# Where the first token columns come from, who casts the weights, and the order of the first FFN pieces

## The chip, the cores and the metric

The kernel runs on one core of one Trainium2 chip. The metric is the device time of one execution in microseconds (us), and lower is better. An execution is called slow here when it is over 1.5% above the fastest one of the same kernel; ratios use fast runs alone. "The profile" is one execution recorded by the hardware profiler. PE is TensorE, DVE is VectorE, ACT is ScalarE, POOL is GpSimd, SP is SyncE; a q after a name (SPq, ACTq) is that engine issuing a DMA.

## The reference, cut to what matters

```python
# q, k, v: (8 batches, 8 heads, 576 tokens, 64), float32
q_s = softmax(q, axis=features)
k_s = softmax(k, axis=tokens)
kv  = einsum('bhsd,bhde->...', k_s, v)      # one 64x64 matrix per batch and head
x   = einsum('bhsd,bhde->bhse', q_s, kv)    # reshaped to 4608 tokens x 512

logits = x @ w_gate + modality_bias[modality_id]    # 8 experts
e_idx  = argmax(logits)
out    = prob[e_idx] * (relu(x @ w1[e_idx]) @ w2[e_idx])   # 512 -> 1024 -> 512
```

With this draw of inputs the modality bias decides, and only two experts get tokens. The kernel finds the two from the bias at run time, and has a loop for any others that does nothing here.

## The kernel before: the parts that the argument touches

Each batch goes through four steps. Attention makes x. Routing chooses the expert and works out a row number (`place`) for each token. Five *sends* by GpSimd write the token rows into a table `xd` in memory, sorted by expert from both ends. A *fetch* by SP reads 256 rows of the table back, transposed, as the columns `xt` that the FFN multiplies.

```python
def fetch(ph):                                   # ph is the batch
    for slot, lo, w in todo_of(ph):              # two passes: slot 0 and slot 1
        xt, d = fetch_x(lo, w)                   # SP, transposing DMA: xt <- xd
        after(d, part_of[ph], "rows are sent before they are read")
        ti, d = fetch_info(lo, w)                # SP, small rows: gate and token id
        ...
        got[lo] = (xt, ti)

def main_pieces():                               # the FFN, as one stream of pieces
    late = []
    for ph in range(NPH):
        for slot, lo, w in todo_of(ph):
            xt, ti = got.pop(lo)
            ...
            yield from ffn1(w, slot, xt, hT)     # 4 pieces: h_ps, 8 products each
            late.append((ph, lo, w, slot, hT, ti))
            if len(late) > 1 or (ph, slot) == (0, 0):
                yield from second(*late.pop(0))  # 4 pieces: y_ps, 4 products each
```

`mains(n)` emits the next n pieces. `weave(side, rate)` runs attention and routing, and after each of their steps adds `rate` times the step's weight to an account; for each whole unit in it one piece is emitted. The order in which instructions are emitted is the order in which an engine runs them:

```python
alone(route(0)); fetch(0)
cast_weights(0, 0, nc.scalar)
load_weights(eids[1], 1, nc.scalar, (0, 1))      # second expert, from ACT
... attention 1, casts, loads of parts 2 and 3 ...
alone(route(1)); fetch(1)
cast_weights(0, 3, nc.scalar)
load_batch(2, "k", nc.scalar)
cast_weights(1, 0, nc.scalar)
cast_weights(1, 1, nc.vector)
load_batch(2, "v", nc.scalar)
mains(4)
cast_weights(1, 2, nc.scalar)
load_batch(2, "q", nc.scalar)
mains(2)
cast_weights(1, 3, nc.vector)
mains(4)
p2 = prep(2, nc.scalar)
for _ in range(6):
    mains(1); next(p2, None)                     # 16 pieces so far
weave(chain(attend(2), route(2)), 0.6, prep(3, nc.scalar), 6)
fetch(2)
weave(chain(attend(3), route(3)), 0.5, prep(4, nc.scalar), 4)
for b in range(4, B):
    fetch(b - 1)
    weave(chain(attend(b), route(b)), 0.97, ...)
```

A batch has 16 pieces. Because the second product of a pass runs one pass late, piece 13 is the first that needs the fetched rows of batch 1, and piece 29 the first that needs those of batch 2. Before, 16 pieces stand ahead of attention 2 and 25 ahead of attention 3.

The softmax here doesn't subtract the row's maximum and nothing guards it: scores larger than these inputs give would overflow.

## Time and profile before

| | before |
|---|---|
| median of 3 runs | 283.08 us (281.9 to 288.72) |
| span of the first profile; granted TensorE clock | 275.2 us; 0.93 |
| TensorE busy | 192.0 us, 70% of the span |
| kvT of batch 1 (end of the first hole) | 42.63 us |
| first FFN product | 51.25 us |
| first product of batch 1's rows; wait before it | 66.76 us; 2.6 us |
| logits of batch 3; wait for the third fetch just ahead of them | 108.69 us; 8.6 us |

Times of day count from the span's start. The lines themselves are in the prediction. A timeline line has start, duration, engine, source line, operation, tiles and count; in brackets stand the idle time of the engine before it and what ended it.

Before was profiled a second time near the end of the study: span 277.7 us, of the fast state, clock 0.94. Below, "the second profile of before" is this one.

### The profile page before, as it was taken

What the parts mean: (1) busy time and instruction counts of PE and PEld (TensorE: products, weight loads), DVE (VectorE), ACT (ScalarE), POOL (GpSimd) and SP (SyncE); (2) the same over time, 40 slices, a digit from 0 to 9 for tenths busy, and PEclk for the clock granted to TensorE, in tenths of its full rate; (3) what the DMA queues carried; (4) which work ended last, traced back from release to release, by engine and by line L of the source; (5) the groups of instructions that cost most, each with busy time, mean ns of one, the idle gap of its engine ahead of it and who ended that gap; (6) DMA issues with size and microseconds to landing.
All of it is one profiled execution on the core that took longest, in us unless ns stands there. A gap on an engine that the chain in (4) does not pass through costs nothing.

```text
span 275.2 us, 4856 instructions
## 1 busy us (share of the span) xinstructions
PE 192.0 (70%) x1769; PEld 131.3 (48%) x1790; DVE 128.3 (47%) x434; ACT 117.6 (43%) x153; POOL 97.0 (35%) x150
## 2 busy tenths in 40 slices
PE   0255604596996714799899289979989879999700
PEld 0244504464664403556656055746746556665400
DVE  1456805840268510964864445485694202223420
ACT  2268503655977151738358016912513333331100
POOL 7040610651034510370406725256347512223400
PEclk9999999998998975999999759999999999999975
DMA  7999999999987797399978762913613693211200
GB/s 182 361 380 403 392 409 285 279 321 248 312 312 254 293 304 159 128 346 263 163 278 278 295 112 82 156 62 109 156 48 119 139 220 108 79 76 71 78 18 0
DMA packets 46170, 56.94 MB, mean 207 GB/s; under 512 B 27227, under 2 KB 27243, under 8 KB 46140
## 3 DMA queue, kind: packets, MB, share of 16 engines
q10 hardware_dynamic: 11104, 25.43, 27.1%
q1 hardware_dynamic: 30076, 16.39, 25.4%
q0 software_dynamic: 4960, 14.74, 15.4%
q8 instruction: 16, 0.26, 0.4%
q14 instruction: 14, 0.11, 0.1%
HBM read 36.84 MB, written 15.25 MB: 189 GB/s over the span
## 4 chain that ended last, share of the span: by engine, by line
PE 45%; DMA 22%; DVE 18%; issue 5%; ACT 3%; POOL 1%; SPq 0%; another core or an unknown queue 0%; DVEq 0%; POOLq 0%; ACTq 0%
PE h_ps L664 20%; PE y_ps L681 15%; DMA xt<-xd 9%; DMA xd<-xb,place 5%; DMA st<-in_q_dram 5%; DVE xb L462 4%; PE tp_ps L388 3%; DMA st<-in_moe_w_dram 3%; PE kv_ps L355 2%; DVE y_sb L691 2%; PE x_ps L451 2%; PE lg_ps L417 2%; ACT et L316 2%; DVE lg L483 1%; POOL xd L564 1%
## 5 line engine op out<-in xcount | busy, mean ns | idle before, releaser
L664 PE MATMUL h_ps<-xt,W 128*128 128x256 bf16 (+1 forms) x640 | 81.0, 284 | 22.8 <-DMA xt<-xd 20.0
L671 ACT ACTIVATE hT<-h_ps 128x512 bf16<-128x512 f32 x76 | 44.8, 599 | 84.7 <-PE h_ps L664 75.5
L664 PEld LDWEIGHTS <-W 128*128 128x128 bf16 x640 | 61.7, 104 | 35.6 <-DMA xt<-xd 12.6
L681 PE MATMUL y_ps<-W,hT 128*128 128x512 bf16 x283 | 72.1, 382 | 1.2 <-issue 0.2
L694 POOL DMA_INDIRECT out_dram<-y_sb,ix x38 | 38.3, 1007 | 74.7 <-DVE y_sb L691 61.1
L691 DVE TENSOR_SCALAR y_sb<-y_ps,ti 128x512 f32<-128x512 f32 x38 | 28.5, 750 | 51.0 <-PE y_ps L681 46.0
L564 POOL DMA_INDIRECT xd<-xb,place x40 | 39.7, 992 | 30.8 <-DVE et L318 10.0
L681 PEld LDWEIGHTS <-hT 128*128 128x128 bf16 x304 | 27.7, 98 | 27.4 <-issue 0.6
L462 DVE TENSOR_TENSOR xb<-x_ps,qi 128x512 bf16<-128x512 f32 (+1 forms) x40 | 25.6, 675 | 2.9 <-PE x_ps L451 2.6
L451 PE MATMUL x_ps<-kvbd,et 128*128 128x128 bf16 (+1 forms) x160 | 17.6, 253 | 7.5 <-DVE xb L462 7.5
L355 PE MATMUL kv_ps<-vb,ek 64*128 64x129 bf16 x288 | 13.4, 244 | 12.0 <-DVE vb L318 12.0
L336 ACT ACTIVATE eq<-st 128x1152 bf16<-128x1152 f32 x16 | 18.5, 1170 | 5.7 <-DMA st<-in_q_dram 5.7
L336 ACT ACTIVATE ek<-st 128x1152 bf16<-128x1152 f32 x16 | 17.9, 1158 | 4.2 <-DMA st<-in_k_dram 4.2
L451 PEld LDWEIGHTS <-et 128*128 128x128 bf16 (+1 forms) x160 | 12.6, 116 | 13.7 <-DVE xb L462 8.5
L509 POOL TENSOR_TENSOR na<-valid,isa 128x5 f32<-128x5 f32 x8 | 1.6, 199 | 47.6 <-DVE isa L498 47.6
L355 PEld LDWEIGHTS <-ek 64*128 64x128 bf16 x288 | 10.2, 108 | 16.7 <-issue 16.4
L388 PE MATMUL tp_ps<-ident,eq 128*128 128x128 bf16 x144 | 13.3, 242 | 6.2 <-DVE kvbd L376 3.1
L316 ACT COPY et<-tp_ps 128x1024 bf16<-128x1024 bf16 x8 | 8.1, 1012 | 19.0 <-PE tp_ps L388 19.0
L316 ACT CAST vb<-st 128x1152 bf16<-128x1152 f32 x14 | 15.9, 1153 | 0.0
L388 PEld LDWEIGHTS <-eq 128*128 128x128 bf16 x144 | 10.5, 109 | 11.2 <-ACT eq L336 3.4
L316 ACT CAST W<-st 128x2048 bf16<-128x2048 f32 x6 | 11.3, 1892 | 0.0
L408 PE MATMUL g_ps<-wg_sb,kvT 128*128 128x8 bf16 x32 | 2.0, 169 | 12.7 <-ACT kvT L404 12.7
(111 smaller groups left out, 134.8 us busy)
## 6 DMA issues: line engine op xcount, KB each, us to landing
st<-in_k_dram ACTq DMA_DIRECT2D x6, 1152.0 KB, 6.9
st<-in_v_dram ACTq DMA_DIRECT2D x6, 1152.0 KB, 9.7
st<-in_q_dram ACTq DMA_DIRECT2D x6, 1152.0 KB, 8.3
st<-in_moe_w_dram SPq DMA_DIRECT2D x4, 1024.0 KB, 15.1
st<-in_moe_w_dram ACTq DMA_DIRECT2D x4, 1024.0 KB, 13.4
st<-in_k_dram SPq DMA_DIRECT2D x2, 1152.0 KB, 9.5
st<-in_v_dram SPq DMA_DIRECT2D x2, 1152.0 KB, 12.8
st<-in_q_dram SPq DMA_DIRECT2D x2, 1152.0 KB, 14.2
```

What stands on the lines that cost most here:

```text
L316: nc.scalar.copy(out=out, in_=in_)
L336: nc.scalar.activation(out=view((eks if nm == "k" else eqs)[b], [[Dh, 2], [HG * Dh, NJ], [1, Dh]], 2 * g * Dh), in_=src[:, 2 * g : 2 * g + ...
L355: nc.tensor.matmul(out=kv[hg][:, 130 * hp : 130 * hp + 129], lhsT=ek[rows, j, P * hp : P * hp + P], rhs=vb[rows, j, hp, 0:129], start=(j = ...
L388: nc.tensor.transpose(out=view(tp, [[2 * nj * 64, 2], [1, 64]], hp * nj * 64 + jj * 64), in_=eq[:, c0 + jj, P * hp : P * hp + P], identity ...
L451: nc.tensor.matmul(out=view(x_ps, [[2 * Dh, 2], [1, Dh]], (4 * (p_ % 2) + p_ // 2) * Dh, (0, T)), lhsT=et[:, p_, tcol[t] : tcol[t] + T], r ...
L462: nc.vector.tensor_tensor(out=view(xb, [[2 * Dh, HG], [Dh, 2], [1, Dh]], t * RW, (0, T)), in0=view(x_ps, [[2 * Dh, HG], [Dh, 2], [1, Dh]], ...
L564: w = nc.gpsimd.indirect_dma_start(out=xd, out_offset=bass.IndirectOffsetOnAxis(ap=place[0:T, t : t + 1], axis=0), in_=xb[0:T, t, :], in_o ...
L664: nc.tensor.matmul(out=h_ps[:, f * w : (f + 1) * w], lhsT=W[:, slot, kd * F + (f0 + f) * P : kd * F + (f0 + f + 1) * P], rhs=xt[:, kd, 0:w ...
L671: nc.scalar.activation(out=hT[:, f0 : f0 + nf, 0:w], in_=view(h_ps, [[w, nf], [1, w]]), func=ACT.Relu)
L681: nc.tensor.matmul(out=y_ps, lhsT=hT[:, kf, t * P : (t + 1) * P], rhs=W[:, slot, W2 + kf * D : W2 + (kf + 1) * D], start=(kf == 0), stop=( ...
L691: nc.vector.tensor_scalar(out=y_sb, in0=y_ps, scalar1=gate[:, t, 3:4], scalar2=None, op0=ALU.mult)
L694: store = nc.gpsimd.indirect_dma_start(out=out, out_offset=bass.IndirectOffsetOnAxis(ap=ix[:, t : t + 1], axis=0), in_=y_sb, in_offset=Non ...
```

## The change

The intent: the first two FFN passes need not wait for the trip of batch 0's rows through memory, since the rows are still in on-chip memory. A 0/1 matrix built from the row numbers, multiplied from the right, sorts and transposes them at once. ACT no longer issues weight loads, which held its queue for 9 us. Casts are spread over three engines. The order of pieces around attention 2 is changed with it.

```diff
+    def sort_first():
+        xb = xb_b[0]
+        for side in range(2):
+            xt = xpass.tile([P, KD, GW], BF16, name="xt"); firsts.append(xt)
+            ... for half, kd, t: 40 products
+                nc.tensor.matmul(out=s_ps[:, kd, :], lhsT=xb[0:T, t, ...],
+                                 rhs=perms[side][0:T, t, :], ...)
+            copy_on(nc.vector if half else nc.scalar, xt[...], s_ps)
 # in route, ahead of the sends:
+        if ph == 0:
+            ... pl2 = place, as floats, once for each side
+            for side in range(2): for t in range(NT):
+                nc.vector.tensor_scalar(out=pm[:, t, :], in0=iota_p,
+                    scalar1=pl2[:, side, t:t+1], op0=ALU.is_equal)
 # in fetch: for ph == 0 only the small rows are fetched, xt = firsts[slot]
 # schedule (cut):
-    load_weights(eids[1], 1, nc.scalar, ...)     # from ACT, in two portions
+    load_weights(eids[1], 1, nc.sync)            # from SP, at the start
+    cast_weights(0, 0, nc.gpsimd)
     alone(route(0))
-    fetch(0)
     ...
+    sort_first()
     alone(a1)
     alone(route(1))
-    fetch(1)
-    cast_weights(0, 3, nc.scalar); load_batch(2, "k", nc.scalar)
-    cast_weights(1, 0, nc.scalar); cast_weights(1, 1, nc.vector)
-    load_batch(2, "v", nc.scalar)
-    mains(4)
-    cast_weights(1, 2, nc.scalar); load_batch(2, "q", nc.scalar)
-    mains(2)
-    cast_weights(1, 3, nc.vector)
-    mains(4)
+    fetch(0)
+    cast_weights(0, 3, nc.scalar); cast_weights(1, 0, nc.vector)
+    mains(4)
+    load_batch(2, "kv", nc.scalar)
+    cast_weights(1, 1, nc.vector); mains(2)
+    cast_weights(1, 2, nc.vector); mains(2)
+    cast_weights(1, 3, nc.vector)
+    fetch(1)
+    mains(4)
+    load_batch(2, "q", nc.scalar); mains(2)
     p2 = prep(2, nc.scalar); six times: mains(1), one step of p2
-    weave(chain(attend(2), route(2)), 0.6, ...)
+    weave(chain(attend(2), route(2)), 0.5, ...)
```

The biases come by one descriptor onto one partition and are spread by four tiny products. The new order puts 20 pieces ahead of attention 2 and 28 ahead of attention 3.

More of the change, by code (lines that the diff above doesn't have):

```diff
@@ L133 @@
     load_batch(0)
+    bias_1 = const.tile([1, 2, E], FP32)
+    nc.gpsimd.dma_start(
+        out=bias_1,
+        in_=bass.AP(tensor=moe_modality_bias.tensor, offset=moe_modality_bias.offset, ap=[[2 * E, 1], [E, 2], [1, E]]),
+    )
     bias_b = const.tile([P, 2, E], FP32)
-    nc.gpsimd.dma_start(
-        out=bias_b,
-        in_=bass.AP(tensor=moe_modality_bias.tensor, offset=moe_modality_bias.offset, ap=[[0, P], [E, 2], [1, E]]),
-    )
     wg_f = hbuf.tile([P, KF, GW], BF16, name="hT").bitcast(FP32)
@@ L201 @@
     nc.gpsimd.tensor_copy(out=ktf, in_=kt_i)
+    iota_p = const.tile([P, GW], BF16)
+    nc.gpsimd.iota(iota_p, pattern=[[1, GW]], base=0, channel_multiplier=0, allow_small_or_imprecise_dtypes=True)
     sid_i = const.tile([P, NSL], I32)
@@ L230, in gating @@
     def gating():
-        bmx = const.tile([P, 2], FP32, name="bmx")
-        nc.vector.reduce_max(out=bmx, in_=bias_b, axis=AX.X)
-        beq = const.tile([P, 2, E], FP32, name="beq")
-        nc.vector.tensor_tensor(out=beq, in0=bias_b, in1=view(bmx, [[1, 2], [0, E]]), op=ALU.is_ge)
-        nc.vector.tensor_tensor(out=beq, in0=beq, in1=view(wrow, [[0, 2], [1, E]]), op=ALU.mult)
-        nc.vector.reduce_max(out=key, in_=beq, axis=AX.X)
-        same = const.tile([P, 1], FP32, name="same")
@@ L240, in gating @@
-        nc.vector.tensor_tensor(out=same, in0=key[:, 0:1], in1=key[:, 1:2], op=ALU.is_equal)
-        nc.vector.tensor_sub(out=key[:, 1:2], in0=key[:, 1:2], in1=same)
+        bmx = const.tile([1, 2], FP32, name="bmx")
+        nc.vector.reduce_max(out=bmx, in_=bias_1, axis=AX.X)
+        beq = const.tile([1, 2, E], FP32, name="beq")
+        nc.vector.tensor_tensor(out=beq, in0=bias_1, in1=view(bmx, [[1, 2], [0, E]]), op=ALU.is_ge)
+        nc.vector.tensor_tensor(out=beq, in0=beq, in1=view(wrow, [[0, 2], [1, E]], 0, (0, 1)), op=ALU.mult)
@@ L242, in gating @@
+        key_1 = const.tile([1, 2], FP32, name="key_1")
+        nc.vector.reduce_max(out=key_1, in_=beq, axis=AX.X)
+        same = const.tile([1, 1], FP32, name="same")
+        nc.vector.tensor_tensor(out=same, in0=key_1[:, 0:1], in1=key_1[:, 1:2], op=ALU.is_equal)
+        nc.vector.tensor_sub(out=key_1[:, 1:2], in0=key_1[:, 1:2], in1=same)
         nc.vector.tensor_scalar(
-            out=same, in0=key[:, 1:2], scalar1=0.0, scalar2=float(E), op0=ALU.is_equal, op1=ALU.mult
+            out=same, in0=key_1[:, 1:2], scalar1=0.0, scalar2=float(E), op0=ALU.is_equal, op1=ALU.mult
@@ L244, in gating @@
         )
-        nc.vector.tensor_add(out=key[:, 1:2], in0=key[:, 1:2], in1=same)
+        nc.vector.tensor_add(out=key_1[:, 1:2], in0=key_1[:, 1:2], in1=same)
         nc.vector.tensor_scalar(
-            out=eid_i, in0=key[0:1, :], scalar1=-1.0, scalar2=float(E), op0=ALU.mult, op1=ALU.add
+            out=eid_i, in0=key_1, scalar1=-1.0, scalar2=float(E), op0=ALU.mult, op1=ALU.add
         )
+        nb = 2 * E
+        parts = const.tile([1, 4, nb], BF16, name="parts")
+        left = const.tile([1, nb], FP32, name="left")
@@ new lines, in gating @@
+        b1 = view(bias_1, [[1, nb]])
+        nc.vector.tensor_copy(out=parts[:, 0, :], in_=b1)
+        nc.vector.tensor_sub(out=left, in0=b1, in1=parts[:, 0, :])
+        nc.vector.tensor_copy(out=parts[:, 1, :], in_=left)
+        nc.vector.tensor_sub(out=parts[:, 2, :], in0=left, in1=parts[:, 1, :])
+        nc.vector.tensor_copy(out=parts[:, 3, 0:2], in_=key_1)
+        b_ps = sp_ps.tile([P, 2 * nb], FP32, name="b_ps", tag="sp")
+        for i in range(3):
+            nc.tensor.matmul(
+                out=b_ps[:, 0:nb], lhsT=ones[0:1, :], rhs=parts[:, i, :], start=(i == 0), stop=(i == 2)
+            )
@@ L250, in gate_weights @@
+        nc.tensor.matmul(out=b_ps[:, nb : nb + 2], lhsT=ones[0:1, :], rhs=parts[:, 3, 0:2], start=True, stop=True)
+        nc.vector.tensor_copy(out=view(bias_b, [[1, nb]]), in_=b_ps[:, 0:nb])
+        nc.vector.tensor_copy(out=key, in_=b_ps[:, nb : nb + 2])
     def gate_weights():
@@ L467, in x_out @@
         )
-    lws, qis, part_of = {}, {}, {}
+    lws, qis, part_of, perms = {}, {}, {}, []
+    def sort_first():
+        xb = xb_b[0]
+        for side in range(2):
+            xt = xpass.tile([P, KD, GW], BF16, name="xt")
+            firsts.append(xt)
+            for half in range(2):
+                s_ps = mm.tile([P, 2, GW], FP32, name="s_ps", tag="mm")
+                for kd in range(2):
+                    for t in range(NT):
+                        T = tsz[t]
+                        nc.tensor.matmul(
+                            out=s_ps[:, kd, :],
+                            lhsT=xb[0:T, t, (2 * half + kd) * P : (2 * half + kd + 1) * P],
+                            rhs=perms[side][0:T, t, :],
+                            start=(t == 0),
+                            stop=(t == NT - 1),
+                        )
+                copy_on(nc.vector if half else nc.scalar, xt[:, 2 * half : 2 * half + 2, :], s_ps)
+    firsts = []
     ROWS = "rows of their own"
@@ L547, in route @@
         nc.vector.tensor_tensor(out=place, in0=sl, in1=aoff[:, o : o + C], op=ALU.add)
+        if ph == 0:
+            pl2 = small.tile([P, 2, NT], FP32, name="pl2")
+            nc.vector.tensor_tensor(out=pl2[:, 0, :], in0=sl, in1=aoff[:, 0:NT], op=ALU.add)
+            nc.vector.tensor_scalar_add(out=pl2[:, 1, :], in0=pl2[:, 0, :], scalar1=-float(NSLOT - GW))
+            for side in range(2):
+                pm = hbuf.tile([P, KF, GW], BF16, name="hT")
+                perms.append(pm)
+                for t in range(NT):
+                    nc.vector.tensor_scalar(
+                        out=pm[:, t, :], in0=iota_p, scalar1=pl2[:, side, t : t + 1], scalar2=None, op0=ALU.is_equal
+                    )
         nc.vector.scalar_tensor_tensor(
@@ L647, in fetch @@
         for slot, lo, w in todo_of(ph):
-            xt, d = fetch_x(lo, w)
-            after(d, part_of[ph], "rows are sent before they are read")
+            if ph:
+                xt, d = fetch_x(lo, w)
+                after(d, part_of[ph], "rows are sent before they are read")
+            else:
+                xt = firsts[slot]
             ti, d = fetch_info(lo, w)
@@ L757 @@
     gating()
-    p0, p1 = prep(0, nc.vector), prep(1, nc.scalar)
+    p0, p1 = prep(0, nc.vector), prep(1, nc.vector)
     alone(p0)
     eids = nc.values_load_multi_w_load_instructions(
-        eid_i[0:1, 0:2],
-        engines=[ENG.SP, ENG.Activation],
-        min_val=0,
-        max_val=E - 1,
-        skip_runtime_bounds_check_because=WHY,
+        eid_i[0:1, 0:2], engines=[ENG.SP], min_val=0, max_val=E - 1, skip_runtime_bounds_check_because=WHY
     )[1]
     load_weights(eids[0], 0, nc.sync)
+    load_weights(eids[1], 1, nc.sync)
     a0 = attend(0)
@@ L774 @@
     biases()
-    next(a0)
+    next(p1)
+    next(p1)
     alone(a0)
     alone(p1)
+    cast_weights(0, 0, nc.gpsimd)
     alone(route(0))
-    fetch(0)
-    cast_weights(0, 0, nc.scalar)
-    load_weights(eids[1], 1, nc.scalar, (0, 1))
     a1 = attend(1)
@@ L785 @@
     cast_weights(0, 1, nc.scalar)
-    load_weights(eids[1], 1, nc.scalar, (2, 3))
+    sort_first()
     alone(a1)
@@ L789 @@
     alone(route(1))
-    fetch(1)
-    cast_weights(0, 3, nc.scalar)
-    load_batch(2, "k", nc.scalar)
-    cast_weights(1, 0, nc.scalar)
-    cast_weights(1, 1, nc.vector)
-    load_batch(2, "v", nc.scalar)
+    fetch(0)
+    cast_weights(0, 3, nc.scalar)
+    cast_weights(1, 0, nc.vector)
+    mains(4)
+    load_batch(2, "kv", nc.scalar)
+    cast_weights(1, 1, nc.vector)
+    mains(2)
+    cast_weights(1, 2, nc.vector)
+    mains(2)
+    cast_weights(1, 3, nc.vector)
+    fetch(1)
     mains(4)
-    cast_weights(1, 2, nc.scalar)
     load_batch(2, "q", nc.scalar)
     mains(2)
-    cast_weights(1, 3, nc.vector)
-    mains(4)
     p2 = prep(2, nc.scalar)
@@ L805 @@
         next(p2, None)
-    weave(chain(attend(2), route(2)), 0.6, prep(3, nc.scalar), 6)
+    weave(chain(attend(2), route(2)), 0.5, prep(3, nc.scalar), 6)
     fetch(2)
```

## The prediction

> **What bounds the kernel now.** I read the busy rows and slices first, then the chain of waits in order of time, then the timeline of the first 110 us, which is the part that the change edits.
>
> ```profile
> PE 192.0 (70%) x1769; PEld 131.3 (48%) x1790; DVE 128.3 (47%) x434; ACT 117.6 (43%) x153; POOL 97.0 (35%) x150
> ...
> PE   0255604596996714799899289979989879999700
> ...
> PEclk9999999998998975999999759999999999999975
> DMA  7999999999987797399978762913613693211200
> ```
>
> A slice is 6.88 us. From about 160 us on TensorE is the limit; before that no compute engine is. Asked in stretches, TensorE is busy 8.8 of 20 us at 20 to 40, 12.3 at 40 to 60, 13.1 at 80 to 100 and 11.1 at 100 to 120. The DMA row is full to about 82 us. The chain says which waits end last:
>
> ```profile
> 33.52 9.11 DMA st<-in_moe_w_dram
> 42.63 0.59 ACT kvT L404
> ...
> 56.53 4.05 DMA xd<-xb,place
> 60.71 6.00 DMA xt<-xd
> 66.76 5.06 PE h_ps L664 x32
> ...
> 91.72 4.81 DMA xd<-xb,place
> 96.72 10.27 DMA xt<-xd
> 107.03 1.86 PE h_ps L664 x8
> ```
>
> Three holes: 9.1 us that end in a weight load, and twice a round trip of rows to memory and back, transposed (10.1 us for the second batch, 15.1 us for the third). The timeline shows whose hole the first is and what starts the FFN:
>
> ```profile
> 33.13 0.98 POOL L564 DMA_INDIRECT xd<-xb,place  x1 [0.30 <-DVE kvbd L376]
> 33.52 9.07 ACTq L292 DMA_DIRECT2D st<-in_moe_w_dram  x2
> ...
> 40.54 1.34 SPq L609 DMA_TRANSPOSE xt<-xd  x1
> ...
> 42.63 0.59 ACT L404 COPY kvT<-kvT_ps 128x512 bf16<-128x512 bf16 x1 [7.74 <-DMA st<-in_moe_w_dram]
> ...
> 51.25 5.96 PE L664 MATMUL h_ps<-xt,W 128*128 128x256 bf16 x32 [2.86 <-DVE xb L462]
> ```
>
> ACT issues the second expert's weights itself, and its queue stands behind the second of two issues from 33.5 to 42.6; the small copy kvT behind it, ready since 33.3, holds the whole second batch. The first FFN product (51.25) then waits not for its fetched columns but for the vector engine to empty a PSUM buffer of batch 1 (xb L462). So the new source of columns pays only through what else it frees.
>
> **What the Trainium skill says.** (1) "DMA: Bandwidth & Descriptors", section "Issuing engines are not separate DMA queues": issuing elsewhere saves sequencer time only, not bandwidth. The trace agrees: with loads from SP alone the rate was 383 GB/s (10 to 20 us), with sends beside them and ACT's loads queued 402 (20 to 40). (2) "TensorE: Matmul & The Clock Gate", Part 1 and "Back-to-back issue gap": half rate until some 3.4 us of work, then N/2.4 ns. The trace agrees: 32 products of 256 columns take 5.96 us at 51.25 and 5.06 at 66.76, both after an idle stretch, and 3.49 us late in the run (109 ns each). (3) "SBUF — State Buffer", section "Who interferes with whom": GpSimd shares a port pair with the vector engine as an exclusive lock, and vector operations with two SBUF inputs are hit. The trace of before has no long GpSimd cast beside such operations. (4) "GPSIMD Engine Reference", section 3.1: 1.03 to 1.8 cycles an element at 1.2 GHz for a one-input loop. The trace has 2.02 us for a strided cast of 1024 elements (y_sb L216), slower than that.
>
> **The change part by part.**
>
> *Biases by one descriptor.* The bias load lands at 8.26 and its choice of experts ends at 10.02. With one descriptor I estimate [...]five more small vector operations (0.2 us each), four tiny products and two copies. But SP is busy issuing loads until 10.63, and some 7 MB stand ahead of the weights at about 400 GB/s. Gain: 0 to 0.5 us.
>
> *Weights issued by SP only, both experts at once.* Removes ACT's 9.1 us. Without it kvT starts near 33.4 instead of 42.63: minus 9.2 us on the path to the first FFN. The DMA was full anyway, so the bytes come little earlier.
>
> *First cast on GpSimd, ahead of batch 0's routing.* The first weight part left SP at 11.62 and such parts took 13.4 to 15.4 us to land: 25.0 to 27.0. A cast of 2048 elements is 1.8 to 3.1 us by the skill's rates, 4.0 by L216; I take 3.0, ending about 29. Routing's first GpSimd operation (na) ran at 27.05 and the vector engine's next (sl) at 27.72, so routing slips by about 2 us, and by 3 if the lock holds its two-input operations as well. Cost: 2 us.
>
> *Permutations.* Two small operations and ten comparisons of 256 bf16 on the vector engine, ahead of four of the five xb evictions. A vector cast of 2048 elements takes 1.22 us, small operations come each 0.2 us: 12 x 0.2 = 2.4 us. Cost: 2.4 us.
>
> *Products.* 2 sides x 4 column blocks x 5 tiles = 40 products of 256 columns, ahead of kvT on TensorE. By the 5.06 to 5.96 us that 32 took from cold, 6.3 to 7.5 us straight; half of that length warm if the transposes before have warmed it. Four evictions of 0.6 to 0.75 us mostly lie beside. kvT's own transposes had slack there. Cost: 6 us.
>
> Sum for the head: 33.4 + 2 + 2.4 + 6 = 43.8 against 42.63 for kvT. The first FFN product follows kvT by 8.6 us as before: about 52.4 instead of 51.25, plus 1.2 us, uncertain by 2. The removed stall is spent almost whole on the new work in the same chain.
>
> *Fetches.* Two of 20 transposing fetches go (40.5 to 44.4), so the queue is emptier when batch 1 returns; loads of batch 2 now come after the first pass's relus. The fetch of batch 1, which took 6.0 us and left TensorE idle 2.6 us at 64.2, should leave under 1 us. Pass 2 then follows without an idle stretch and runs nearer 3.6 than 5.06 us. Gain: 1.8 + 1.4 = 3.2 us.
>
> *Casts.* ACT loses three casts of 1.89 us, the vector engine gains two of 1.22 us and batch 1's two v casts (0.76 us each). ACT is free when relus begin; neither bounds the stretch. Gain: about 0.
>
> *Order.* Twenty FFN pieces instead of 16 stand before attention of batch 2, and 8 instead of 9 are woven into it, so 28 instead of 25 lie before attention 3. The first piece needing batch 2's fetch therefore comes early in attention 3, and ACT's loads for batch 5 (at 95.6 and 96.5 before, just over the 10.27 us fetch) fall behind it. The fetch then should take about 6 us as at 60.71: minus 4.3 us. Against it, attention 3 has its transposes and logits still to do when the fetch lands, where before only logits stood there: plus 1.5 us.
>
> Sum: +1.2 - 3.2 - 4.3 + 1.5 = -4.8 us. After 160 us TensorE is full and the gain is carried to the end unchanged; the last hole (5.5 us at 216) moves with it. 283.1 - 4.8 = 278.3 us; I say 278.5.
>
> **The rivals.**
>
> *A: the head really gets shorter.* If GpSimd's cast ends by 27.5 and the products run warm (4.4 us), kvT stands at 40 and everything is 4 us earlier: 272 to 275 us. For it: the stall is the largest single hole of the chain, and the waiting engines are idle there. Against it: GpSimd's one comparable cast was slow.
>
> *B: a new wait in place of the old.* The lock and the cast hold batch 0's routing for 4 to 5 us, and attention 3, stuck at the third batch's fetch, becomes the late chain: 283 to 287 us. For it: routing is two-input vector operations from end to end, and GpSimd's queue is in order. Against it: TensorE has FFN work of batch 1 left to fill with.
>
> *C: absorbed.* The stages at 140 to 160 us wait for a send and a fetch again (5.6 and 3.1 us); a lead won before can be lost there, leaving 281 to 284 us. For it: the same loads and sends follow. Against it: sends follow attention, which is ordered among the FFN pieces, so a lead moves them too.
>
> **Range and chances.** The middle sum is minus 1.7%. The head's uncertainty of 2 us and that of the third fetch of 3 us, with the three runs of before spread from 281.9 to 288.7 us, give 271.5 to 285.5 us for 8 in 10. Faster by over 2% needs less than 277.4 us, so A or a fuller effect of the order: 0.40. Within 2%: 0.52. Slower needs B and more: 0.08.
>
> **What would show it right or wrong.** In the profile of the changed kernel: ACT's hole at 33.5 gone (right) and in its place routing of batch 0 behind a GpSimd cast of W of about 3 us; comparisons of 0.2 us; 40 products in 5 to 7 us; the first FFN product between 50 and 54.5 us; under 1 us of waiting for batch 1's fetch; a fetch of batch 2 of about 6 us. The prediction is wrong if the first FFN product comes before 49 us (A), if it comes after 55 or if attention 3 ends much later than the fetch (B), or if the lead at 110 us is over 4 us and gone at 200 (C).

## The result, and the profile after

The changed kernel took 305.03 us (median of 4 runs, 301.15 to 307.72) against 284.53 us for before (4 runs). The ratio is 1.0708 with a 95% interval of 1.0528 to 1.0888: slower. A ratio in this text is the mean time of one kernel's fast runs over the mean of before's fast runs of the same rounds, so it is not quite the ratio of the medians. The profile of after is of a slow run (307.72 us, clock 0.88); its fast runs had 0.884 to 0.894, so little separates them.

These are the page's busy line and slices of after. A slice is a fortieth of the span, 7.65 us.

```profile
PE 213.3 (70%) x1813; PEld 142.1 (46%) x1834; DVE 136.9 (45%) x459; ACT 111.1 (36%) x150; POOL 100.2 (33%) x152
...
PE   0455793939975449587973986798598499999900
...
PEclk9999996695999756979997899599899869999975
DMA  7999970295997834749976933511502384221200
```

TensorE's share is the same 70%, but it is 70% of a span 31 us longer. In the DMA row stands a 0 at the seventh slice (46 to 54 us) and weak slices behind it, where the row of before was full to 82 us: loads that had filled that stretch were moved to a later one.

The following table sets the milestones of the second profile of before against after, and against the run with before's head and only the new order of pieces (an experiment below).

| milestone (us) | before, second profile | after | new order alone |
|---|---|---|---|
| first FFN product | 52.09 | 53.93 | 51.08 |
| attention 2's kv begins | 68.86 | 82.15 | 82.40 |
| logits of batch 2 | 78.36 | 90.77 | 91.02 |
| logits of batch 3 | 101.39 | 121.08 | 120.77 |
| logits of batch 7 | 198.24 | 226.06 | 224.27 |
| end of the span | 277.7 | 306.0 | 306.3 |

Of 28.3 us, 1.8 are there at the first FFN product, 19.7 at batch 3's logits, 27.8 at batch 7's. From there to the end both take the same, 79.5 and 79.9 us.

**The head came out in its range.** The timeline of after, with the cast on GpSimd, one of routing's two-input operations beside it, the comparisons, the products and the first FFN product:

```profile
25.33 1.89 POOL L341 CAST W<-st 128x2048 bf16<-128x2048 f32 x1 [8.33 <-DMA st<-in_moe_w_dram]
25.47 1.77 DVE L543 SCALAR_TENSOR_TENSOR isa<-xb,key,valid 128x5 bf16<-128x5 f32 x1
...
28.73 2.04 DVE L602 TENSOR_SCALAR hT<-iota_p,pl 128x256 bf16<-128x256 bf16 x10
...
34.49 10.41 PE L505 MATMUL s_ps<-hT,xb 64*128 64x256 bf16 x40
...
53.93 5.84 PE L724 MATMUL h_ps<-xt,W 128*128 128x256 bf16 x32 [2.94 <-DVE xb L485]
```

The cast took 1.89 us, less than the 3.0 expected: the low end of the prediction's 1.8 to 3.1 us. A five-element operation of routing that began beside it took 1.77 us, against 0.23 us in before. The ten comparisons took 2.04 us. The 40 products took 10.41 us, far over the expected 6. The PEclk row draws full clock there only because the trace has no clock record before 44.80 us, when the last product runs. Read product by product, the twelve profiles with these products have their first record (full clock) between 35.76 and 44.80 us; before it the products come 235 to 259 ns apart, after it 137 to 151 ns. So their length follows the moment at which the clock rises: with the record at 35.76 they took 6.62 us (e7 below), at 38.36 7.77 (e2), at 44.80 10.41. It differs between executions of one kernel: 7.24 us in e9 and 9.34 us in g2, the same kernel. The first FFN product stands at 53.93, again waiting for an xb eviction.

**TensorE stops for the small rows.** The timeline of after around batch 1's fetch, with ACT's load, SP's small rows and transposing fetch, the vector engine's use of the small rows, and the product that waited:

```profile
59.87 0.42 ACTq L123 DMA_DIRECT2D st<-in_k_dram  x1
...
61.70 0.90 SPq L671 DMA_DIRECT2D ti<-xd  x2
62.77 2.72 SPq L666 DMA_TRANSPOSE xt<-xd  x1
...
68.37 0.16 DVE L687 SCALAR_TENSOR_TENSOR m<-ti,m 128x2 f32<-128x2 int32 x1 [10.84 <-DMA ti<-xd]
...
69.44 5.79 PE L724 MATMUL h_ps<-xt,W 128*128 128x256 bf16 x26 [5.34 <-DVE y_sb L751]
```

The small rows of batch 0 (`ti`) are issued after batch 1's sends are waited for, at 61.70, though they had been ready long before. The vector engine waits 10.84 us for them, the FFN's evictions `y_sb` wait behind it, and TensorE stops 5.34 us until 69.44. Counted in products, the stop falls inside batch 0's second pass, between pieces 9 and 10; the first product of batch 1's rows (piece 13) comes at 74.59 and doesn't wait.

**Attention 3 is cut in two.** The timeline of TensorE round the third fetch, in before and then in after:

```profile
89.52 1.23 PE L355 MATMUL kv_ps<-vb,ek 64*128 64x129 bf16 x28
91.66 0.40 PE L355 MATMUL kv_ps<-vb,ek 64*128 64x129 bf16 x8
...
107.03 1.86 PE L664 MATMUL h_ps<-xt,W 128*128 128x256 bf16 x8 [8.58 <-DMA xt<-xd]
108.69 0.72 PE L417 MATMUL lg_ps<-gx,et 128*128 128x18 bf16 x20
```

```profile
100.96 1.70 PE L378 MATMUL kv_ps<-vb,ek 64*128 64x129 bf16 x28
...
110.23 1.87 PE L724 MATMUL h_ps<-xt,W 128*128 128x256 bf16 x8 [7.57 <-DMA xt<-xd]
112.03 0.61 PE L378 MATMUL kv_ps<-vb,ek 64*128 64x129 bf16 x8
...
121.08 0.65 PE L440 MATMUL lg_ps<-gx,et 128*128 128x18 bf16 x20
```

The second profile of before has the order of the first, but no wait at that product:

```profile
100.52 1.03 PE L664 MATMUL h_ps<-xt,W 128*128 128x256 bf16 x8
101.39 0.65 PE L417 MATMUL lg_ps<-gx,et 128*128 128x18 bf16 x20
```

So the wait of 8.58 us, which the prediction read, isn't in every execution of before.

In before attention 3's 36 kv products end ahead of the wait for `xt`, and the whole chain of its transposes runs beside the fetch; the logits follow the waiting product by 1.7 us. In after the waiting product stands between 28 and 8 of the kv products. So the 8 that are left, the kv matrix, its transposes and the gate products all start after the fetch, and the logits come 10.85 us behind it. The account of `weave` says why: attention's first three steps weigh 0.7 each, at rate 0.5 that is 1.05, so one piece is emitted after the third step, and with 28 pieces ahead that piece is number 29. With 25 ahead, number 29 is the fourth, and falls just before the logits.

### The profile page after: what moved, and what is told of

Its sections match the earlier page's. It is cut to its first block, busy times and chain, and to the rows that moved or that the text cites.

```text
span 306.0 us, 4967 instructions
## 1 busy us (share of the span) xinstructions
PE 213.3 (70%) x1813; PEld 142.1 (46%) x1834; DVE 136.9 (45%) x459; ACT 111.1 (36%) x150; POOL 100.2 (33%) x152
## 4 chain that ended last, share of the span: by engine, by line
PE 37%; issue 18%; DVE 18%; DMA 8%; another core or an unknown queue 7%; SPq 4%; ACT 3%; POOL 1%; POOLq 0%; DVEq 0%; ACTq 0%
PE h_ps L724 15%; PE y_ps L741 12%; DMA st<-in_v_dram 5%; PE s_ps L505 3%; PE tp_ps L411 3%; DVE xb L485 3%; DVE y_sb L751 2%; SPq L666 2%; PE lg_ps L440 2%; DVE lg L528 1%; POOL xd L621 1%; DMA xt<-xd 1%; DMA out_dram<-y_sb,ix 1%; DVE isa L543 1%
## 5 line engine op out<-in xcount | busy, mean ns | idle before, releaser
L724 PE MATMUL h_ps<-xt,W 128*128 128x256 bf16 (+1 forms) x640 | 89.2, 298 | 21.6 <-DMA xt<-xd 7.6
L724 PEld LDWEIGHTS <-W 128*128 128x128 bf16 x640 | 64.9, 108 | 38.0 <-issue 23.3
L741 PEld LDWEIGHTS <-hT 128*128 128x128 bf16 x304 | 27.9, 98 | 27.7 <-issue 1.0
L411 PE MATMUL tp_ps<-ident,eq 128*128 128x128 bf16 x144 | 16.9, 283 | 23.3 <-DVE kvbd L399 17.9
L411 PEld LDWEIGHTS <-eq 128*128 128x128 bf16 x144 | 13.6, 130 | 26.8 <-DVE kvbd L399 15.5
L474 PE MATMUL x_ps<-kvbd,et 128*128 128x128 bf16 (+1 forms) x160 | 16.0, 235 | 9.0 <-DVE xb L485 9.0
L474 PEld LDWEIGHTS <-et 128*128 128x128 bf16 (+1 forms) x160 | 11.3, 107 | 15.5 <-DVE xb L485 10.0
L378 PE MATMUL kv_ps<-vb,ek 64*128 64x129 bf16 x288 | 14.8, 258 | 1.6 <-DVE vb L341 1.1
L341 DVE COPY et<-tp_ps 128x1024 bf16<-128x1024 bf16 (+1 forms) x16 | 7.8, 489 | 17.7 <-PE tp_ps L411 17.7
L392 DVE TENSOR_SCALAR kinv<-kv_ps 128x2 f32<-128x2 f32 x16 | 1.8, 152 | 28.4 <-PE kv_ps L378 14.5
L339 ACT CAST vb<-st 128x1152 bf16<-128x1152 f32 x12 | 13.8, 1160 | 0.0
```

What stands on the lines that cost most here:

```text
L339: nc.scalar.copy(out=out, in_=in_)
L378: nc.tensor.matmul(out=kv[hg][:, 130 * hp : 130 * hp + 129], lhsT=ek[rows, j, P * hp : P * hp + P], rhs=vb[rows, j, hp, 0:129], start=(j = ...
L411: nc.tensor.transpose(out=view(tp, [[2 * nj * 64, 2], [1, 64]], hp * nj * 64 + jj * 64), in_=eq[:, c0 + jj, P * hp : P * hp + P], identity ...
L474: nc.tensor.matmul(out=view(x_ps, [[2 * Dh, 2], [1, Dh]], (4 * (p_ % 2) + p_ // 2) * Dh, (0, T)), lhsT=et[:, p_, tcol[t] : tcol[t] + T], r ...
L724: nc.tensor.matmul(out=h_ps[:, f * w : (f + 1) * w], lhsT=W[:, slot, kd * F + (f0 + f) * P : kd * F + (f0 + f + 1) * P], rhs=xt[:, kd, 0:w ...
L741: nc.tensor.matmul(out=y_ps, lhsT=hT[:, kf, t * P : (t + 1) * P], rhs=W[:, slot, W2 + kf * D : W2 + (kf + 1) * D], start=(kf == 0), stop=( ...
```

## The experiments

All 18 computed the output correctly. Each is told with before's runs on the same chip. A name ends with the median, the ratio and its interval. Lines with minus and plus are against the kernel named.

### First round: the small rows, the order, or the head (before 283.95 us, 7 runs)

My theory was that the small rows' late issue starts the loss; the rival was that the order alone does it.

**e1_info_early**, against after:

```diff
     alone(route(0))
+    fetch(0)          # small rows at once
 ...                    # cut: the columns are put in after sort_first()
     alone(route(1))
-    fetch(0)
```

> The changed kernel with the small rows (gate and row number) of the first passes fetched right after routing of batch 0 instead of after routing of batch 1. Theory T1 (the 10.8 us wait of the first output row index for these rows, held back by the last send of batch 1, starts the loss and all later stages only inherit it): 8 to 12 us less than the changed kernel, about 293 to 297 us, no wait for ti over 1 us. Theory T2 (the new order of FFN pieces around attention 2 and 3 costs most): 3 us less at most, 300 us or more, and the idle stretches after 100 us stay.

307.3 us, 1.0814 [1.0673, 1.0956]. The first FFN product came 3.5 us earlier, at 50.41 (the 40 products took 6.99 us here), and the wait for the small rows was gone. But the first product of batch 1's rows then waited 11.79 us for its columns, until 74.34: ACT's loads of batch 2's k and v had been issued at 55.70 and 56.23 and q at 62.65, beside the fetch at 61.88. One wait took the other's place. The theory of the small rows falls as the cause of the time.

**e2_old_order**, e1 with before's order of pieces, loads and rate (16 and 25 pieces):

```diff
+    fetch(1)                       # straight after route(1), as before
     ... mains and load_batch(2, ...) as in before ...
-    weave(chain(attend(2), route(2)), 0.5, ...)
+    weave(chain(attend(2), route(2)), 0.6, ...)
```

> As the run before, and the FFN pieces, the loads of batch 2 and the rate of weaving in attention 2 back in the order of the kernel before; permutations, bias, issuing from SP and the split casts stay. T2: 15 to 25 us less than the changed kernel, 280 to 290 us. T1: no better than the run before it by more than 3 us.

289.05 us, 1.0214 [1.0105, 1.0323]. The order, with the loads' places and the rate, gives back about 18 us. About 2% stays: batch 1's product still waited 9.89 us, until 73.71. The vector engine and GpSimd at that place:

```profile
52.10 3.64 DVE L341 CAST W<-st 128x2048 bf16<-128x2048 f32 x3
...
52.73 1.99 POOL L621 DMA_INDIRECT xd<-xb,place  x1 [0.30 <-issue]
```

Three weight casts of expert 1 now stand together on the vector engine, and the send beside them took 1.99 us; in the kernel e7 below, with two of them on ACT, the same send took 1.59 us, and a send beside one such cast in before 1.50 us. This agrees with the Trainium skill, "SBUF — State Buffer", section "Who interferes with whom": a DMA that seems stalled by a vector operation is one whose descriptors GpSimd makes, and it was kept from the port that it shares.

**e3_sp_weights**, against before: both experts' weights from SP at the start, ACT's loads removed.

```diff
     load_weights(eids[0], 0, nc.sync)
+    load_weights(eids[1], 1, nc.sync)
-    load_weights(eids[1], 1, nc.scalar, (0, 1))
-    load_weights(eids[1], 1, nc.scalar, (2, 3))
```

> The kernel before with one thing of the change: both experts' weights issued by SP. If the hole of ACT at 33.5 to 42.6 us is what bounds the head (as predicted), the first FFN product comes near 46 to 48 us (the fetched columns bound it next) and the run gains 2 to 5 us; rival: the loads that move ahead push sends and fetches of batch 0 back, first FFN product at 51 or later and no gain.

293.27 us, 1.0285 [1.0139, 1.0431] (the profile is of a slow run). ACT's hole went, but SP's transposing fetch of batch 0, issued at 45.77, took 6.69 us, and the first FFN product came at 56.16 after a wait of 15.56 us. So the early loads don't pay by themselves here. Whether they do with the permutation products, which do away with that fetch, was not tested apart.

**e4_new_order_alone**, against before: only the order, the loads' places and the rate of the new schedule.

```diff
     alone(route(1))
-    fetch(1)
     cast_weights(0, 3, nc.scalar)
     ... as in the change's schedule, casts left on their old engines ...
+    fetch(1)
     mains(4)
+    load_batch(2, "q", nc.scalar)
+    mains(2)
-    weave(chain(attend(2), route(2)), 0.6, ...)
+    weave(chain(attend(2), route(2)), 0.5, ...)
```

> The kernel before with only the new order: 20 FFN pieces before attention 2, loads of batch 2 after the first pass, weaving at 0.5. T2: 8 to 20 us slower than before, with attention 3 stuck on the third fetch. T1: within 4 us of before (here the small rows of batch 0 are still fetched early).

307.09 us, 1.084 [1.0717, 1.0962]. That is 23 us over before, where 8 to 20 had been expected. The whole loss comes from the order, the loads' places and the rate together, without a permutation in the kernel. The timeline of this run, with ACT's load, the fetch of batch 1 and the product that waited:

```profile
57.67 0.39 ACTq L123 DMA_DIRECT2D st<-in_k_dram  x1
...
61.31 1.43 SPq L609 DMA_TRANSPOSE xt<-xd  x1
...
73.32 2.96 PE L664 MATMUL h_ps<-xt,W 128*128 128x256 bf16 x13 [8.80 <-DMA xt<-xd]
```

The columns come 12.0 us after the issue of the fetch, where in before they came 6.0 us after it. The third fetch then cost another wait of 6.70 us, to 109.92, in the cut attention 3.

TensorE's totals say what kind of time it is. Against the second profile of before, which has the same number of PE records (1790), e4 is busy 207.5 us instead of 198.1, and stands 98.8 us instead of 79.6. So of 28.6 us two thirds are standing, and one third is the same work at a lower clock (0.877 against 0.940).

### Second round: which part of the order, and which mend of the head (before 280.01 us, 7 runs)

**e5_fewer_pieces**, against after: three pieces fewer between the loads and attention 2, so 17 and 25.

```diff
-    for _ in range(6):
-        mains(1)
+    for i in range(6):
+        mains(i % 2)
```

> The changed kernel with three FFN pieces fewer ahead of attention 2 (every other of the last six is left out), so that 25 and not 28 pieces lie ahead of attention 3 and 33 and not 36 ahead of attention 4, as in the kernel before; everything else, the late loads too, stays. Theory 'too many pieces too early' (the first product of each batch's rows is reached before its rows are sent and fetched, and the tensor engine stands in every batch): most of the loss goes, 288 to 295 us, the logits of batch 3 come at 108 to 112 us and not at 121, and the stalls of 4 to 6 us in batches 4 to 7 are gone. Theory 'late loads of batch 2': no change, 302 to 308 us, logits of batch 3 near 120.

290.88 us, 1.0354 [1.0242, 1.0466] (profile of a slow run). About half of the loss is gone, and attention 3's kv is whole again (99.25 and 101.43).

**e6_early_loads**, against after: batch 2's loads close to before's places among the casts.

```diff
+    load_batch(2, "k", nc.scalar)
     cast_weights(1, 0, nc.vector)
+    load_batch(2, "v", nc.scalar)
     mains(4)
-    load_batch(2, "kv", nc.scalar)
     cast_weights(1, 1, nc.vector)
+    load_batch(2, "q", nc.scalar)
 ...
-    load_batch(2, "q", nc.scalar)
```

> The changed kernel with the loads of batch 2 back in their old places (k ahead of expert 1's first cast, v after it, q after the first four pieces); the number of pieces stays at 20. Theory 'late loads': attention 2's first product moves from 82 back to about 72 to 76 us and the time falls to 290 to 296 us. Theory 'too many pieces too early': attention 2 starts at most a few us sooner, the logits of batch 3 stay at 116 to 121 us, and the time stays at 300 to 307 us.

304.24 us, 1.0915 [1.0799, 1.103]. Nothing came back. The vector engine still waited 9.70 us for the small rows, and TensorE 4.86 us, to 67.25: while that wait stands, moving the loads alone shows nothing.

**e7_act_casts**, e2 with expert 1's parts 0 and 2 cast by ACT, as in before:

```diff
-    cast_weights(1, 0, nc.vector)
+    cast_weights(1, 0, nc.scalar)
-    cast_weights(1, 2, nc.vector)
+    cast_weights(1, 2, nc.scalar)
```

> The changed kernel in the old order (run e2_old_order, 289 us), with the casts of parts 0 and 2 of expert 1's weights back on the scalar engine as in the kernel before. Theory 'casts on the vector engine hold up the descriptors of the sends' (one send took 1.99 us instead of 0.98 while three casts ran there): the last send of batch 1 lands 2 to 3 us sooner, pass 2 starts at 68 to 71 us and not at 73.7, and the time is 283 to 287 us. Theory 'the fetch merely shares the DMA engines with the loads of batches 2 and 3': no change, 288 to 290 us, pass 2 at 73 to 75 us.

283.61 us, 1.0033 [0.9888, 1.0178] (profile of a slow run, so its stages are a rough guide). Batch 1's product came at 68.89 after a wait of 6.83 us, 4.8 us earlier than in e2.

**e8_sp_loads**, e2 with batch 2's loads issued by SP, long before the fetch:

```diff
     cast_weights(0, 0, nc.gpsimd)
+    load_batch(2, "k", nc.sync)
     alone(route(0))
 ...
     cast_weights(0, 1, nc.scalar)
+    load_batch(2, "v", nc.sync)
 ...
     cast_weights(0, 2, nc.scalar)
+    load_batch(2, "q", nc.sync)
```

> The changed kernel in the old order (run e2_old_order), with the three loads of batch 2 issued by the sync engine as soon as their buffers are free, in the stretch from 40 to 50 us in which the DMA engines stand idle there. Theory 'the fetch shares the DMA engines with the loads': the loads are over by 55 us, the sends of batch 1 and its fetch find the engines free, pass 2 starts at 64 to 67 us and not at 73.7, and the time is 278 to 284 us. If the fetch is held by something else, pass 2 stays at 71 to 75 us and the time at 287 to 291 us.

279.98 us, 0.9993 [0.9891, 1.0094]. The wait at batch 1's rows fell to 1.22 us, and its product came at 64.21 against 73.71 in e2. In this order, then, the loads that ACT issued ahead of the fetch made the trip long. Two sends were about as slow as in e2 (1.78 and 1.97 us), so the casts beside the sends did not decide it.

### Third round: both mends, and the number of pieces (before 284.44 us, 11 runs)

**e9_both_mends** is e8 with e7's edit.

> Run e8_sp_loads (old order, loads of batch 2 from the sync engine in the idle stretch) with the casts of parts 0 and 2 of expert 1 on the scalar engine as well, as in e7_act_casts. If each of the two mends something of its own (engines free for the fetch; descriptors of the sends not held up), they add: pass 2 at 61 to 64 us, time 274 to 279 us. If both only free the same fetch, or if later batches give the head's gain back whatever it is (batch 3's logits 9.5 us earlier than in the kernel before in e8, batch 7's 1.3 us later): 278 to 283 us.

279.52 us, 0.9814 [0.9695, 0.9933]. No wait is left at batch 1's rows. The time fell in the range of the second theory, and the interval overlaps that of e8 (0.9993), so what the two casts add to e8 isn't shown.

**e10_six_fewer** is e8, and **e11_before_six_fewer** is before, each without the six pieces beside `prep(2)`:

```diff
     for _ in range(6):
-        mains(1)
         next(p2, None)
```

> Run e8_sp_loads with the six pieces left out that go with the casts of batch 2 (10 pieces ahead of attention 2 instead of 16). Theory 'pieces reached before their rows are there': in e8 a batch still takes 24.4 us from batch 4 to 7, with stalls of 1 to 4 us and a half-speed clock after each; with six fewer the first product of a batch's rows comes six pieces later, the stalls go, a batch takes 20 to 22 us and the time is 262 to 272 us. Theory 'a batch takes 24 us because of its own chain of attention and routing': the logits of batch 7 move by no more than the 6 us at the start and the pieces left out are done at the end, 276 to 282 us.

> The kernel before with the same six pieces left out (10 ahead of attention 2). Theory 'pieces reached before their rows are there': its stall of 6.7 us at 153 us and the clock after it go, 270 to 278 us (ratio 0.96 to 0.99); attention 2 starts no sooner than its loads allow, so less than in e10. Rival 'the kernel before has just enough pieces, fewer leave the tensor engine idle in attention 2': 283 to 288 us.

e10: 292.83 us (6 runs, 287.31 to 299.35; their spread gave no ratio). e11: 290.8 us, 1.0252 [1.0173, 1.0331]. I had expected a gain from fewer pieces. Both fell: from batch 7's logits to the end, e10 took 87.7 us and e11 89.1 us, where the second profile of before took 79.5. Pieces left out early are added at the end, and the batches between were not faster for it.

**e12_before_three_more**, against before: 19 and 28 pieces, with every load and fetch where before has it in the order.

```diff
-    for _ in range(6):
-        mains(1)
+    for i in range(6):
+        mains(1 + i % 2)
```

> The kernel before with three pieces more ahead of attention 2 (19 instead of 16; 28 ahead of attention 3 and 36 ahead of attention 4, as in the changed kernel) and nothing else of the change. Theory 'pieces reached before their rows are there': ratio 1.03 to 1.06, batch 3's logits at 113 to 121 us instead of 108.7, and stalls of 3 to 6 us in batches 4 to 7. Rival 'the number of pieces only hurts with the late loads or with the permutations': 0.99 to 1.02.

298.2 us, 1.0527 [1.0399, 1.0656]. The timeline of TensorE in this run:

```profile
88.94 1.65 PE L355 MATMUL kv_ps<-vb,ek 64*128 64x129 bf16 x28
98.82 1.86 PE L664 MATMUL h_ps<-xt,W 128*128 128x256 bf16 x8 [8.23 <-DMA xt<-xd]
100.62 0.62 PE L355 MATMUL kv_ps<-vb,ek 64*128 64x129 bf16 x8
...
109.68 0.65 PE L417 MATMUL lg_ps<-gx,et 128*128 128x18 bf16 x20
```

This is after's picture, made in before by three pieces: kv split in 28 and 8 by the waiting product, logits of batch 3 at 109.68 instead of 101.39 (113 to 121 had been expected). Batch 1's rows were not waited for here, so the number of pieces costs this by itself. Batches 4 to 7 then took 25.9 us each (second profile of before: 24.2).

### Fourth round: is 16 the best number (before 283.86 us, 23 runs)

**f1_one_more** is before with 17 pieces (`mains(1 + (i == 0))`), **f2_two_fewer** before with 14 (`mains(1 - (i % 3 == 0))`).

> The kernel before with one piece more ahead of attention 2 (17 instead of 16), nothing else. If the loss climbs piece by piece (three more cost 5.3%): ratio 1.01 to 1.025. If there is a step, because one piece more already puts the first product of a batch's rows ahead of the wait that decides: 1.035 to 1.06. If only the third piece does it: 0.99 to 1.01.

> The kernel before with two pieces fewer ahead of attention 2 (14 instead of 16). Six fewer cost 2.5%. If 16 is a sharp best place, 1.01 to 1.025; if the time is flat between 10 and 16 with a dip nobody tuned, 0.98 to 1.0.

f1: 285.72 us, 1.0149 [1.0035, 1.0263] (profile of a slow run). f2: 294.2 us, 1.0429 [1.0298, 1.056]. f2's timeline shows what two fewer ran into:

```profile
65.11 0.39 ACTq L123 DMA_DIRECT2D st<-in_v_dram  x1
...
67.00 5.92 SPq L609 DMA_TRANSPOSE xt<-xd  x1
...
75.97 2.32 PE L664 MATMUL h_ps<-xt,W 128*128 128x256 bf16 x10 [10.91 <-DMA xt<-xd]
```

With a piece left out of its first step, `prep(2)` runs earlier, and the loads of batch 3 that it issues (k at 64.29, v at 65.11) fall beside the fetch of batch 1. Its second issue stood 5.92 us in SP's queue, and TensorE waited 10.91 us. It looks like e4's wait again, with another batch's loads; no run without these loads tested it.

**f3_best_lower_rate** is e9 with rate 0.9 instead of 0.97 from batch 4 on; **f4_best_two_fewer** is e9 with 14 pieces, the same edit as f2.

> Run e9_both_mends with 14 instead of 15 pieces woven into each of batches 4 to 7 (rate 0.90 for 0.97). If what a batch loses there hangs on the pieces in it: a batch takes 22 to 23 us instead of 24.4 and the time is 272 to 277 us (e9: 279.5). If a batch's time is set by its own chain of attention, routing and sends: the tail grows by the four pieces that are left over, 280 to 286 us.

> Run e9_both_mends with two pieces fewer ahead of attention 2 (14). If the mended version has room on that side, because its rows arrive sooner: 274 to 279 us. If it falls as e10_six_fewer did (six fewer cost 12 us there): 282 to 288 us.

f3: 286.64 us, 1.0188 [1.0076, 1.03]; the rival held, with 83.1 us behind batch 7's logits against 79.3 in e9. f4: 282.52 us over 20 runs from 276.13 to 296.78, so wide that it has no ratio; it is inconclusive.

### Fifth round: before and the mended version again (before 280.34 us, 11 runs)

**g1_before_again** is before unchanged, **g2_best_again** e9 unchanged, to see which differences belong to the execution.

> The kernel before, unchanged, for a second profile. If the stalls belong to the order of the pieces: no stall between 162 and 219 us, as in the first profile, logits of batches 4 to 7 about 20 to 28 us apart with only one long gap, span 274 to 280 us. If they belong to the single execution: stalls of 4 to 5 us in batches 5 to 7 in this profile, span 283 to 290 us, and the ratio stays at 1.0 either way (0.99 to 1.01).

> Run e9_both_mends again, unchanged. If its lead is real: ratio 0.97 to 0.99 again. If it was luck of that round: 0.99 to 1.01.

g1: 283.39 us (278.53 to 292.46, 4 runs); it is the same kernel, so no ratio is given. g2: 277.38 us, 0.9882 [0.9821, 0.9943], within 2% of before. g2's runs spread from 275.49 to 279.83, before's 11 from 278.21 to 290.28. So the changed kernel with before's order, SP's early loads and two casts back on ACT beats both kernels, by 1 to 2% over before. Which of its parts earns this isn't shown.

g1 also corrected my reading of the later batches. The waits of TensorE from 75 us on, in the first profile of before and in this one (total us, count, longest):

```profile
PE h_ps L664 <- DMA xt<-xd: 17.4, 3, 8.6
PE tp_ps L388 <- DVE kvbd L376: 3.1, 6, 1.6
```

```profile
PE tp_ps L388 <- DVE kvbd L376: 8.4, 4, 5.0
```

The same kernel waits 17.4 us for fetches in one execution; in the other no such row stands among TensorE's waits, and it waits 8.4 us for the kv matrix, once for 5.0. Such stops near the end of a batch's kv products, about 5 us each, were the new order's doing in my theory. Before has them too: in the second profile TensorE gives no semaphore signal for over 3 us six times between 75 and 260 us, for 3.5 to 5.3 us each, 27.6 in all; in after seven times, 44.2 us in all, of which 12.7 at the third fetch. The mended version (g2) has six with 27.7 us, as before has; the first profile of before has three with 22.2 us, e4 eleven with 51.8 and e12 ten with 52.2. So the new order brings more of this time, but before isn't free of it. What they are stays open. Here is one of them in e4, with TensorE's rows, then ACT's, then the vector engine's:

```profile
158.52 0.40 PE L355 MATMUL kv_ps<-vb,ek 64*128 64x129 bf16 x8
158.86 1.05 PE L664 MATMUL h_ps<-xt,W 128*128 128x256 bf16 x8
...
163.87 0.60 ACT L671 ACTIVATE hT<-h_ps 128x512 bf16<-128x512 f32 x1 [10.74 <-remote]
...
163.89 0.23 DVE L369 TENSOR_SCALAR kinv<-kv_ps 128x2 f32<-128x2 f32 x2 [4.40 <-remote]
```

TensorE's kv and h_ps rows are modelled to end by 159.91, but the two engines that wait for its signals start again at 163.87 and 163.89, and in between no row of TensorE stands, nor a wait. It isn't the landing of xt, nor a load of a batch: those are elsewhere in time. I found no more.

## Why the prediction was wrong, by its own steps

- **Biases, weights from SP, cast, permutations, products.** The sum said 52.4 us for the first FFN product, between 50 and 54.5; it was 53.93, and kvT came at 45.28 instead of 43.8. Inside it batch 0's logits came 1.3 us earlier (21.60 against 22.87), the cast cost less (1.89 instead of 3.0 us) and the products more (10.41 instead of 6). The errors have opposite signs, so it was partly luck that the head came out within its range. The expected 5 to 7 us for the products held in three of the twelve profiles that have them (6.62, 6.95 and 6.99 us). Two readings were off without moving the sum: 32 late products took 3.66 us by the measure of the 5.96 and 5.06 beside them, not 3.49, and the hole "5.5 us at 216" is a fetch, for which TensorE waited 2.12 us.
- **Fetches, -3.2.** This step failed. It expected under 1 us of waiting at batch 1's rows. In after that came true only by luck: TensorE had already stood 5.34 us in batch 0's second pass, for small rows that the change fetches behind batch 1's sends, and the prediction had no such wait. It noted that loads of batch 2 "now come after the first pass's relus", but did not see that this puts them beside the fetch: once the small rows come early the wait at batch 1's rows is 11.79 us (e1), and 8.80 us in e4. SP's early loads (e8) bring it to 1.22 us.
- **Order, -4.3 and +1.5.** This step failed too, and by the ratios it cost most (e12 against e5). Its picture was right: piece 29 did come early in attention 3, and the third fetch took 3.2 us in after (107.01 to 110.23), shorter even than the 6 expected. The term "plus 1.5 us" for what attention 3 still had to do was mis-sized: from the waiting product to the logits it took 10.85 us in after against 1.7 in before, so about +9; e12 lost 8.3 us at this place. The profile of before held the number: attention 2 took 8.5 us from its kv (71.75) to its logits (80.22). And the 4.3 us to be saved were not there. They were taken from a wait that the second profile of before doesn't have; in after TensorE still waited 7.57 us, since the fetch itself was issued late (107.01 against 93.40), behind an attention 2 that began at 82.15 and not at 68.86. While it waits TensorE has nothing else to do: the pieces that could have filled the time had been spent already, ahead of attention 2.
- **Where the time went, by place.** Of the 19.7 us at batch 3's logits, 12.4 stand already at batch 2's (90.77 against 78.36), and 7.3 come in attention 3. Of the 13.3 us by which attention 2 begins later, the head's 1.8, the stop of 5.34 and the four pieces done ahead (y_ps, 3.62 us) make 10.8.
- **"Carried to the end unchanged."** Not so: the gap to before grew from 19.7 to 27.8 us over batches 4 to 7. After took 26.2 us a batch there and e12 25.9, both with the too-early pieces, the second profile of before 24.2. The lower clock is part of it; whether the standing brings the lower clock, or how else the early order reaches so far, was not settled. The clock records of after fit the first: half clock begins at 164.27 and 191.57, just behind stops that end at 163.11 and 191.28; but another begins at 130.13, ahead of a stop from 130.96.
- **Rivals.** B named the right chain ("attention 3, stuck at the third batch's fetch, becomes the late chain"), for another reason than its own and with 283 to 287 us much too small. A and C did not come. The chance of slower was given 0.08, since each part was priced by the wait that it removes and none by the fill that it uses up.
- **Permutations.** What they are worth by themselves was not measured. With the order set back, the head's changes together came to 1.0214 (e2), and with two casts back on ACT to 1.0033 (e7): no gain. The versions with less (0.9993 in e8, 0.9814 and 0.9882 in e9 and g2) also have batch 2's loads issued by SP, and before with these loads was not run. Their first FFN product comes at 50.79, 50.61 and 52.81 us, against 51.25 and 52.09 in the two profiles of before: the head is hardly shorter.

How the two causes share the loss is known only roughly. With the pieces' number alone mended, 1.0354 is left (e5); with that number alone spoilt, 1.0527 (e12); with the order alone, 1.084 (e4). The two overlap and don't add: the wait at batch 1's rows also shifts when the third fetch can go.

## What to carry to other kernels

Work that fills waits is a stock: count, for each coming round trip, which piece is the first to need it and what stands behind that piece in the engine's order, and price the whole chain that is stuck behind it, not the length of the wait. When a load is moved, look at what latency-bound transfer it will then run beside. Try such an order by itself, one or two pieces up and down, before bundling it with another change: here 14, 17 and 19 pieces were 4.3%, 1.5% and 5.3% slower than 16, and with 14 a load had moved beside a fetch.

## What the Trainium skill lacked or had wrong

- "TensorE: Matmul & The Clock Gate", Part 1, gives a warm-up of some 3.4 us of sustained work. From the start of the transposes ahead of the 40 products TensorE worked without a break of over 0.3 us, and the first record of the full clock came after 3.0 us (e7), 4.5 (e9), 9.6 (g2, the same kernel as e9) and 12.1 us (after). A warm-up of 3.4 us doesn't explain the last two.
- "Perfetto Trace Analysis", section "Summary: the profiler window per engine type", says that the end of a TensorE row is estimated. Behind rows that end by 159.91 the readers started at 163.87 and 163.89 (e4). No page says what TensorE may be doing in such 4 us.
- "SBUF — State Buffer", section "Who interferes with whom", gives no size for sends beside vector casts: 0.98 us became 1.50 beside one cast (before) and 1.99 beside three (e2).
- No page gives a size for what loads of 1.15 MB each, issued beside a transposing fetch, do to it: 6.0 us from issue to use (before) became 12.0 us (e4), and 1.2 us of waiting was left when the loads went out early (e8).
